# A scheduled attention-and-experts kernel: the loop's head moved behind all scatters, half of the early low parts on GpSimd, the last block closed tile by tile, and other due times

## The chip, the core and the metric

The kernel runs on one core of a Trainium2 chip. The core has a matrix engine (TensorE, PE in the profile; PEld is its loading of weights), a vector engine (DVE), a scalar engine (ACT), GpSimd (POOL) and a queue engine for transfers (SP). Times are device microseconds of the core; the figure that counts is the median of several runs. One execution more is taken with the hardware profiler, and all rows below come from it.

## The reference

Attention over 8 batches of 576 positions with 8 heads of 64, where four heads see a local window and four see a stride of 32; then a mixture of 8 experts over the 4608 rows of 512, each row going to one expert:

```
scores = scale * q @ k.T                      # (8, 8, 576, 576), scale = 1/8
masks  = (0 <= rel < 32) for heads 0..3;  (rel >= 0 and same position mod 32) for heads 4..7
attn   = softmax(where(masks, scores, -1e9)) @ v
x      = attn as 4608 rows of 512
expert = argmax(x @ w_gate);  gate = its softmax probability
out[row] = gate * (relu(x[row] @ w1[expert]) @ w2[expert])   # w1 512x1024, w2 1024x512
```

Everything is float32. A product is made of three matmuls on a high and a low part of each factor (hi*hi, hi*lo, lo*hi), so weights and rows are first split into a high part (a cast on ACT) and a low part (a subtraction).

## The kernel before

**Attention.** Each batch has five banks of scores, 40 in all. A bank goes from PE (mask and scores, `mask`, `scores`) to DVE (`big`, `minus`), ACT (`expo`), DVE (`total`), GpSimd (`norm`, line 664), back to PE (`turned`, four transposes) and to ACT (`out_`); then PE multiplies with v (`av_mm`) into the PSUM banks v and w. Two batches form a group of 9 row tiles. Of each group the gate logits are made (`logit_ops`, whose copy `ev`, line 822, is on DVE), each row tile is transposed and written to a DRAM table xd (`row_ops`, through the PSUM tags in `XTAGS`), and `route_ops` makes the lists of rows of each expert, whose last matmuls are `lists`.

**Experts.** `window` is one block: some 128-row tiles of one expert, gathered from xd by indirect DMAs of GpSimd, transposed on PE into a bank (`tr`, line 421, four transposes of a column of tiles, one after another in `vtags`), split by ACT (`hi`, tile xh) and DVE (`lo`, tile xl), multiplied with w1 (`mm1`, lines 449 to 451, eight steps j of 12 matmuls), relu on ACT (hh), its low part on DVE (hl), multiplied with w2 (`mm2`, lines 469 to 471) into one bank per tile, scaled by the gate (`fin`, tiles y) and written to the output rows by an indirect DMA of GpSimd (`scatter_rows`, line 347, with a one-element memset ahead of a scatter that follows another). A chunk of weights (`weights`) is a load of 1 MB on SP, then for each of its two halves a cast on ACT (line 330) and a subtraction on DVE (line 333, wlo): the first half belongs to w1, the second to w2.

Four early blocks (`PHASES`: experts 0, 2, 4, 6, two tiles each) take rows of the first two groups, and their work lies between the banks of the second half of the attention. After the last group come `make_ids`, `slot_tables` (DVE, lines 1057 to 1087) and the lists of extra tiles ("slots", eight planned by `SLOTS`), then the late blocks of experts 0 to 7 (two or four tiles each) with the slots between them. A slot uses the bank v for its transposes (line 1156), as the late blocks do. At the end a loop takes whatever slots are left over (here it runs no turn).

**What sets the order.** Every piece of work is an `Op` with an engine, a cost, dependences, buffers (`Token`s) and a due time `pri`. `Plan.run` lays them out greedily: for each engine it takes, of the operations that could start within `LOOK` of the earliest, the one with the smallest due time (a PE operation of another tile form counts `FORM_COST` later). Due times come from the constants at the top: `PACE` and `PACE2` for the banks, `LEAD` for loads, `WLEAD` and `WSPL` for weights and their splits, `GLEAD` for gathers, `TLEAD` for a block's transposes, `SLOTP` and `BASEP` for slot tables and late blocks. The order so found is what each engine runs; on the chip an engine takes its instructions in that order and waits at each for its semaphores.

Of the kernel before, what the change touches and what calls it, by code (L numbers as in the profile page):

```python
# [7 lines left out]
F32 = mybir.dt.float32  # L8
# [34 lines left out]
XTAGS = ("yy", "yy", "vw", "vw")  # L43
# [5 lines left out]
PACE = 5.69  # L49
PACE2 = 4  # L50
LAG = 5.0
LEAD = 48.87
ROWLAG = 2.0
FILL0 = 4.87
FILLW = 40.13
WLEAD = 20.91
WSPL = 3.63
SLOTP = 1987.69
BASEP = 2000.0
GLEAD = 38.84  # L60
TLEAD = 22.28
# [38 lines left out]
FORM_COST = 1.14  # L100
LOOK = 0.3
# [17 lines left out]
class Plan:  # L119


    def __init__(self, bufs):
# [12 lines left out]
        self.hold = True  # L135

# [3 lines left out]
    def add(self, eng, cost, fn, deps=(), pri=0.0, take=(), give=(), form=FULL, nbytes=0, rate=380e3, ins=1):  # L140
# [66 lines left out]
    def run(self, held=False):  # L207
# [5 lines left out]
        for op in ops:  # L213
            for d in op.deps:
# [7 lines left out]
        while must:  # L222
# [26 lines left out]
            for s in op.succ:  # L249
                s.left -= 1  # L250
                if s.left == 0:
                    s.at = max(d.done for d in s.deps)
                    avail[s.eng].append(s)
# [15 lines left out]
def moe_attn(ctx, tc, lqk, vl, sqk, vs, wg, wcat, blob, out):  # L269
# [14 lines left out]
                 "route": 1, "sl": 2, "xge": 4, "xe": 1, "ye": 2, "xgm": 9, "xtm": 2, "yp": 5, "sx": 2, "shr": 2, "shh": 2,  # L284
# [76 lines left out]
    def weights(source, deps, pri, pools, after_row=None):  # L361
# [11 lines left out]
        ld = add(SP, 0.45, load, deps, pri, take=[traw], nbytes=128 * CHW * 4)  # L373
        parts = []
        for h in range(2):
# [12 lines left out]
            d = add(DVE, 1.23, lo, [a], pri + WLEAD - WSPL + 0.2 * h, give=[traw])  # L388
# [3 lines left out]
    def window(e, nt, idc, odc, deps, pri, pace, gp, xp, yp_, names, pools, rows=N + 1, width=512, vtags="vw", ytags=YTAGS):  # L392
# [6 lines left out]
        for t in range(nt):  # L399
# [6 lines left out]
            gs.append(add(POOL, 1.0, g, deps, pri - GLEAD, take=[tk], nbytes=128 * XW * 4, rate=250e3))  # L406
# [3 lines left out]
        for dc in range(4):  # L410
# [18 lines left out]
            p = before = add(PE, 0.109 * nt, tr, gs + [before], pri - TLEAD + 2.5 * dc, take=[tv] + ([txx] if dc == 0 else []), ins=2 * nt)  # L429
# [4 lines left out]
        prev = []  # L434
        last = None
        for c in range(NCH):
            p0 = pri + 2 * c * pace
            w, parts, twhl = weights(lambda e=e, c=c: wcat[(e * NCH + c) * 128:(e * NCH + c + 1) * 128, :], (), p0 - WLEAD, pools)
            for fl in range(2):
# [22 lines left out]
                def mm2(w=w, fl=fl, j=j, b=b):  # L462
# [3 lines left out]
                    for t in range(nt):  # L466
                        ts = slice(t * 128, (t + 1) * 128)
                        yb = st["yb"][t]
                        nc.tensor.matmul(yb, b["hh"][:, ts], w["hi"][:, s], start=(j == 0), stop=False)  # L469
                        nc.tensor.matmul(yb, b["hh"][:, ts], w["lo"][:, s], start=False, stop=False)  # L470
                        nc.tensor.matmul(yb, b["hl"][:, ts], w["hi"][:, s], start=False, stop=(j == 7))  # L471

                m1 = add(PE, 12 * mm, mm1, los + [parts[0]], pri + j * pace, take=[tt], give=[txx], ins=24)
                r = add(ACT, act_cost(n), relu, [m1], pri + j * pace, take=[th])
                d = add(DVE, dve_cost(n), rest, [r], pri + j * pace, give=[tt])
                last = add(PE, nt * 3 * 0.229, mm2, [d, parts[1], last], pri + (j + 1.5) * pace, take=ty if j == 0 else (),
                           give=[th, twhl], ins=6 * nt)
        for t in range(nt):
# [11 lines left out]
            f = add(eng, 0.69 if eng == DVE else 0.62, fin, [last], pri + 8 * pace - 8, take=[tk], give=[ty[t], tg[t]])  # L490
# [6 lines left out]
    with ExitStack() as actx:  # L497
# [310 lines left out]
        def logit_ops(g, c3, p):  # L808
# [11 lines left out]
            def ev():  # L820
                st["ls"] = rt.tile([128, 384], F32, name="ls", bufs=2)
                nc.vector.tensor_copy(out=st["ls"], in_=st["lb"][:, 0:384])
# [27 lines left out]
            a = add(DVE, 0.56, ev, [a], p, take=[tls], give=[tb1])  # L850
# [40 lines left out]
        def route_ops(g, p, reds):  # L891
# [47 lines left out]

            def am_():  # L940
# [431 lines left out]
```

## Time and profile before

| | |
|---|---|
| median of three runs | 713.14 us (711.83 to 713.17) |
| profiled execution, its time | 707.22 us |
| profiled execution, span from first to last instruction | 705.4 us |
| PE busy in the span | 642.0 us, 91% |
| DVE, ACT, POOL busy | 449.0, 350.6, 149.2 us |
| mean granted TensorE clock | 0.954 of full speed |

The engine with the largest busy share is PE. A matmul's end in the profile is modelled, so PE's busy time is read for where it is missing: a stretch's idle time of PE and the share of the clock that was granted in it (a level of 0.5 is 1.2 GHz, 1.0 is 2.4 GHz) say what the stretch loses.

### The profile page before, as it was taken

How to read it: one execution, taken by the hardware profiler on the slowest of the kernel's cores; microseconds unless marked ns; L12 is line 12 of the kernel's file. 1: busy time of each engine (PE TensorE's matmuls, PEld its weight loads, DVE VectorE, ACT ScalarE, POOL GpSimd, SP SyncE). 2: the span in 40 equal slices, each digit the busy share in tenths (PEclk: the TensorE clock that was granted, in tenths of full speed). 3: DMA queues.
4: the chain of work that ended last, by engine and by line, in shares of the span. 5: the costliest groups of instructions: out<-in, count | busy, mean ns of one | idle time of the engine just before them, and what ended most of it. 6: DMA issues, size and time to landing. Idle time of an engine off the chain costs nothing. (4 is left out here: it accounts for less than half of the span.)

```text
span 705.4 us, 16723 instructions
## 1 busy us (share of the span) xinstructions
PE 642.0 (91%) x7013; PEld 542.1 (77%) x7020; DVE 449.0 (64%) x791; ACT 350.6 (50%) x601; POOL 149.2 (21%) x189
## 2 busy tenths in 40 slices
PE   5788879799999888999999999999799999999991
PEld 3666656688788677988888888888698888898880
DVE  4576867664886769995455676566477555687110
ACT  2454555355475654464444665446366555676110
POOL 1222321410322414110102403021502200332002
PEclk9699999699999999999999999999899999999996
DMA  9887666826574466576344859565655854592001
GB/s 348 348 304 287 219 234 206 292 102 219 198 257 160 150 258 250 207 261 250 129 178 165 291 200 341 207 238 199 238 179 196 295 196 168 185 369 86 15 1 61
DMA packets 31949, 149.65 MB, mean 212 GB/s; under 512 B 4861, under 2 KB 4861, under 8 KB 21632
## 3 DMA queue, kind: packets, MB, share of 16 engines
q1 hardware_dynamic: 19584, 118.24, 46.5%
q0 software_dynamic: 6432, 20.26, 8.1%
q10 hardware_dynamic: 5856, 10.07, 3.8%
q8 instruction: 56, 0.92, 0.5%
q14 instruction: 21, 0.17, 0.1%
HBM read 129.38 MB, written 20.22 MB: 212 GB/s over the span
## 5 line engine op out<-in xcount | busy, mean ns | idle before, releaser
L333 DVE TENSOR_TENSOR wlo<-raw,whi 128x1024 fp32r<-128x1024 f32 x160 | 195.0, 1235 | 53.8 <-ACT whi L330 53.3
L330 ACT CAST whi<-raw 128x1024 fp32r<-128x1024 f32 x160 | 164.6, 1048 | 22.3 <-PE y L471 10.9
L449 PE MATMUL t<-xh,whi 128*128 128x256 f32 (+1 forms) x384 | 127.3, 332 | 0.0
L451 PE MATMUL t<-xh,wlo 128*128 128x256 f32 (+1 forms) x384 | 123.0, 320 | 0.0
L450 PE MATMUL t<-xl,whi 128*128 128x256 f32 (+1 forms) x384 | 122.6, 319 | 0.0
L456 ACT ACTIVATE hh<-t 128x256 fp32r<-128x256 f32 (+1 forms) x96 | 43.7, 456 | 121.1 <-PE t L451 112.2
L459 DVE SCALAR_TENSOR_TENSOR hl<-t,hh 128x256 fp32r<-128x256 f32 (+1 forms) x96 | 48.5, 508 | 77.4 <-ACT hh L456 77.0
L469 PE MATMUL y<-whi,hh 128*128 128x512 f32 x192 | 79.4, 414 | 2.0 <-ACT hh L456 2.0
L450 PEld LDWEIGHTS t<-xl,whi 128*128 128x128 f32 x384 | 73.3, 191 | 5.9
L449 PEld LDWEIGHTS t<-xh,whi 128*128 128x128 f32 x384 | 73.2, 191 | 6.0
L451 PEld LDWEIGHTS t<-xh,wlo 128*128 128x128 f32 x384 | 73.1, 190 | 5.7
L471 PE MATMUL y<-whi,hl 128*128 128x512 f32 x192 | 76.1, 396 | 0.5 <-DVE hl L459 0.5
L470 PE MATMUL y<-wlo,hh 128*128 128x512 f32 x192 | 75.5, 393 | 0.0
L664 POOL TENSOR_TENSOR prob<-prob,ri 128x512 f32<-128x512 f32 x40 | 43.2, 1083 | 141.6 <-DVE ri L660 70.1
L347 POOL DMA_INDIRECT out_dram<-y,soids x8 | 11.5, 1439 | 205.2 <-DVE y L357 204.9
L643 DVE TENSOR_REDUCE nm<-s 128x8 f32<-128x512 f32 x40 | 27.3, 683 | 34.2 <-PE s L618 23.2
L471 PEld LDWEIGHTS y<-whi,hl 128*128 128x128 f32 x192 | 36.2, 188 | 9.8 <-DVE hl L459 1.5
L347 POOL DMA_INDIRECT out_dram<-y,oids x24 | 29.9, 1245 | 57.4 <-DVE y L357 43.5
L469 PEld LDWEIGHTS y<-whi,hh 128*128 128x128 f32 x192 | 36.2, 189 | 7.6 <-ACT hh L456 2.2
L470 PEld LDWEIGHTS y<-wlo,hh 128*128 128x128 f32 x192 | 36.4, 190 | 5.5
L652 ACT ACTIVATE prob<-prob 128x512 f32<-128x512 f32 x40 | 25.4, 634 | 27.2 <-DVE prob L648 26.1
L327 ACT COPY pT<-t 128x512 f32<-128x512 f32 x40 | 23.0, 590 | 29.0 <-PE t L670 27.0
(166 smaller groups left out, 1255.1 us busy)
## 6 DMA issues: line engine op xcount, KB each, us to landing
raw<-in_wcat_dram SPq DMA_DIRECT2D x80, 1024.0 KB, 5.4
xd<-xr ACTq DMA_DIRECT2D x36, 264.0 KB, 4.4
lqk_sb<-in_lqk_dram SPq DMA_DIRECT2D x16, 592.0 KB, 6.4
sqk_sb<-in_sqk_dram SPq DMA_DIRECT2D x16, 576.0 KB, 6.1
vt<-in_vl_dram SPq DMA_DIRECT2D x16, 576.0 KB, 6.6
vst<-in_vs_dram SPq DMA_DIRECT2D x8, 704.0 KB, 4.6
xg<-xd,ids POOLq DMA_INDIRECT x24, 4.5
out_dram<-y,oids POOLq DMA_INDIRECT x24, 5.0
```

Source lines behind the costliest of these rows:

```text
L330: nc.scalar.copy(out=hi, in_=src)
L333: nc.vector.tensor_tensor(out=lo, in0=src, in1=hi.bitcast(F32), op=ALU.subtract)
L347: i = nc.gpsimd.indirect_dma_start(out=out, out_offset=bass.IndirectOffsetOnAxis(ap=idc, axis=0), in_=y, in_offset=None, bounds_check=N - ...
L449: nc.tensor.matmul(hb[:, 0:n], w["hi"][:, s], xh[:, dc, :], start=(dc == 0), stop=False)
L450: nc.tensor.matmul(hb[:, 0:n], w["hi"][:, s], xl[:, dc, :], start=False, stop=False)
L451: nc.tensor.matmul(hb[:, 0:n], w["lo"][:, s], xh[:, dc, :], start=False, stop=(dc == 3))
L456: nc.scalar.activation(out=b["hh"][:, 0:n], in_=b["hb"][:, 0:n], func=AF.Relu)
L459: nc.vector.scalar_tensor_tensor(out=b["hl"][:, 0:n], in0=b["hb"][:, 0:n], scalar=0.0, in1=b["hh"][:, 0:n].bitcast(F32), op0=ALU.max, op1= ...
L469: nc.tensor.matmul(yb, b["hh"][:, ts], w["hi"][:, s], start=(j == 0), stop=False)
L470: nc.tensor.matmul(yb, b["hh"][:, ts], w["lo"][:, s], start=False, stop=False)
L471: nc.tensor.matmul(yb, b["hl"][:, ts], w["hi"][:, s], start=False, stop=(j == 7))
L664: nc.gpsimd.tensor_tensor(out=pv, in0=pv, in1=st["ri"].unsqueeze(2).broadcast_to([128, 8, 64]), op=ALU.mult)
```

## The change

Named pieces, in the order of the diff:

- Other numbers in the table of due times, `FORM_COST` and `LOOK`; `XTAGS` now puts every group's row transposes on the banks v and w, where groups 0 and 1 used the two y banks.
- Operations may be given a `row`: those of one row keep the order in which they are added (gathers of one pool, loads of one pool, transposes, `mm1`, `mm2`).
- In `weights`, a half that is named in `side` has its low part made on GpSimd; the early blocks name the second half (`EARLY_SIDE = (1,)`). That is one half of each of 16 chunks.
- In `window`, the block of expert 7 has `tail=True`: its last two `mm2` steps (j = 6 and 7) are laid out tile by tile, and a tile's scaling waits for its own last matmul only.
- The logits' copy goes to ACT (`LS_ENG`). `POOL_ROUTES` is empty, so the edits in `route_ops` only divide `bb_` in two.
- Slots gather into a pool of their own (`xgs`, 2 buffers); `xgm` has 7 buffers where it had 9.
- A late block that follows an early expert's block (experts 1, 3, 5, 7) transposes through the banks v, s, s, v and not through v alone.
- `region.close()` stands behind the loop, so the region in which the order is set by hand takes in the loop too.

```diff
-XTAGS = ("yy", "yy", "vw", "vw")
+XTAGS = ("vw",) * 4
...
-PACE = 5.69
-PACE2 = 4
+PACE = 5.08
+PACE2 = 4.89
...
-WSPL = 3.63
-SLOTP = 1987.69
+WSPL = 0.6
+SLOTP = 2008.12
...
-GLEAD = 38.84
-TLEAD = 22.28
+GLEAD = 5
+TLEAD = 24.93
+EW = 128 * max(n for _, _, n in PHASES)
+LS_ENG = "ACT"
+POOL_ROUTES = ()
+EARLY_SIDE = (1,)
...
         op.hold = self.hold
+        op.behind = self.last.get(row) if row else None
+        if row:
+            self.last[row] = op
...
-            def lo(sl=sl):
-                split_lo(w["raw"][:, sl], w["hi"][:, sl], w["lo"][:, sl])
+            le = POOL if h in side else DVE
+
+            def lo(sl=sl, le=le):
+                if le == POOL:
+                    nc.gpsimd.tensor_tensor(out=w["lo"][:, sl], in0=w["raw"][:, sl], in1=w["hi"][:, sl].bitcast(F32),
+                                            op=ALU.subtract)
+                    scattered[0] = False
+                else:
+                    split_lo(w["raw"][:, sl], w["hi"][:, sl], w["lo"][:, sl])
...
+                if tail and j >= 6:
+                    steps.append((mm2, d, parts[1], th, twhl))
+                    th.users = nt
+                    twhl.users = 2 * nt
+                    continue
...
+        ends = [last] * nt
+        if tail:
+            for t in range(nt):
+                for k, (mm2, d, part, th, twhl) in enumerate(steps):
+                    last = add(PE, 3 * 0.229, lambda mm2=mm2, t=t: mm2([t]), [d, part, last], pri + 8.5 * pace + 0.1 * t,
+                               give=[th, twhl], ins=6)
+                ends[t] = last
...
-            f = add(eng, 0.69 if eng == DVE else 0.62, fin, [last], pri + 8 * pace - 8, take=[tk], give=[ty[t], tg[t]])
+            f = add(eng, 0.69 if eng == DVE else 0.62, fin, [ends[t]], pri + 8 * pace - 8, take=[tk], give=[ty[t], tg[t]])
...
-    xgm = ctx.enter_context(tc.tile_pool(name="xgm", bufs=9))
+    xgm = ctx.enter_context(tc.tile_pool(name="xgm", bufs=7))
+    xgs = ctx.enter_context(tc.tile_pool(name="xgs", bufs=2))
...
-               bpools[:1] if ns else bpools, vtags="v")
+               bpools[:1] if ns else bpools, vtags="vss" if 0 < ENT.get(e - 1, 0) else "v", tail=e == E - 1)
...
     plan.run()
-    region.close()
 
     nslots = nc.values_load(nsl[0:1, 0:1], min_val=0, max_val=MAXSLOT)
     with tc.For_i(RSLOT, nslots, 1) as s:
...
         scatter_rows(y, cols[1])
+    region.close()
```

**Place A, the late block of expert 4 among the work of expert 3 and the slots, PE.** In the order before, its first two transposes (line 421, tiles of xg into v) stand around those of a slot (line 1156), all three in the one bank v:

```order
L1217 MATMUL w_6579<-whi_6675,shl_6784 128x512
L421 MATMUL v_6824<-cst_82,xg_6280 128x128
L421 MATMUL v_6824<-cst_82,xg_6803 128x128
L1156 MATMUL v_6839<-cst_82,xg_6810 128x128 x4
L421 MATMUL v_6860<-cst_82,xg_6280 128x128
L421 MATMUL v_6860<-cst_82,xg_6803 128x128
L1187 MATMUL t_6863<-whi_6745,sxh_6837 128x256
```

In the changed kernel the block's first transposes (line 437) are followed by 18 matmuls before a slot's (line 1198), and those by 12 before the block's next; the first fence is the block's first, the second the slot's:

```order
L467 MATMUL t_6639<-xh_6000,wlo_6576 128x512
L437 MATMUL v_6660<-cst_82,xg_5928 128x128
L437 MATMUL v_6660<-cst_82,xg_6291 128x128
L1257 MATMUL w_6606<-whi_6532,shh_6633 128x512
L1258 MATMUL w_6606<-wlo_6533,shh_6633 128x512
```

```order
L1231 MATMUL t_6674<-whi_6630,sxl_6315 128x256
L1198 MATMUL v_6693<-cst_82,xg_6555 128x128 x4
L485 MATMUL y_6323<-whi_6430,hh_6599 128x512
L486 MATMUL y_6323<-wlo_6431,hh_6599 128x512
L487 MATMUL y_6323<-whi_6430,hl_6600 128x512
```

So three uses of the bank v that stood back to back now have matmuls of other blocks between them.

**Place B, the passage from attention to the late blocks, DVE.** Before, `slot_tables` (22 instructions, lines 1057 to 1087) stand ahead of the low parts xl of the early block of expert 6, whose four pairs of transposes PE makes without a matmul between; here the last four rows of the tables and what follows:

```order
L1084 TENSOR_SCALAR raw_4627<-raw_4627 128x40
L1085 TENSOR_TENSOR skey_97<-raw_4627 128x40
L1086 TENSOR_SCALAR raw_4627<-raw_4627 128x40
L1087 CAST srow_96<-raw_4627 128x40
L333 TENSOR_TENSOR xl_4667<-v_4668,xh_4666 128x256
L333 TENSOR_TENSOR xl_4667<-w_4674,xh_4666 128x256
L459 SCALAR_TENSOR_TENSOR hl_4651<-t_4605,hh_4650 128x256
```

In the changed kernel the same 22 instructions (lines 1099 to 1129) stand later, between the low parts hl of two steps of that early block:

```order
L1127 TENSOR_TENSOR skey_97<-raw_4783 128x40
L1128 TENSOR_SCALAR raw_4783<-raw_4783 128x40
L1129 CAST srow_96<-raw_4783 128x40
L475 SCALAR_TENSOR_TENSOR hl_4815<-t_4770,hh_4814 128x256
L342 TENSOR_TENSOR wlo_4818<-raw_4710,whi_4817 128x1024
L342 TENSOR_TENSOR xl_4821<-v_4822,xh_4820 128x256
```

What now waits behind the tables is hl of the step that PE made as t_4770 (and the first xl of the late block of expert 0), where it was the four xl of expert 6.

**Place C, the end of the program, POOL.** One piece of the difference; the rows with + are the changed kernel's last scatters and the loop's head, those with - the order before, where two scatters stand behind the loop's code. The gather and the scatter of a "dyn" tile are the loop's body:

```order
-L1256 COMPARE_AND_BRANCH
-L1256 UNCONDITIONAL_BRANCH
-L347 DMA out_dram<-y,oids 4608x512
-L346 MEMSET gap 1x1
-L347 DMA out_dram<-y,oids 4608x512
-L1368 UNCONDITIONAL_BRANCH
-L1368 ISA
```

```order
+L355 MEMSET gap 1x1
+L356 DMA out_dram<-y,oids 4608x512
+L1296 TENSOR_LOAD nsl
+L1297 COMPARE_AND_BRANCH
+L1297 ISA
+L1297 UNCONDITIONAL_BRANCH
```

The last two scatters moved from behind the loop to ahead of its head.

## Rows read from the trace of the kernel before

**Rows 1.** The page's first part: busy us, share of the span, instructions.
```profile
PE 642.0 (91%) x7013; PEld 542.1 (77%) x7020; DVE 449.0 (64%) x791; ACT 350.6 (50%) x601; POOL 149.2 (21%) x189
```

**Rows 2.** Table by stage: stretch, length, busy by engine, PEclk granted, DMA.
```profile
7.00:140.00 133.00, 107.60 (x2825) 85.02 (x2827) 93.09 (x231) 60.70 (x128) 36.84 (x49) 0.87 0.78 281
140.00:240.00 100.00, 96.40 (x1641) 79.67 (x1647) 69.55 (x153) 58.74 (x118) 23.31 (x33) 0.99 0.52 179
240.00:285.00 45.00, 39.59 (x306) 33.48 (x307) 35.56 (x91) 22.59 (x41) 16.55 (x22) 0.92 0.70 254
285.00:490.00 205.00, 204.18 (x1181) 176.90 (x1180) 135.10 (x170) 107.72 (x163) 30.06 (x31) 1.00 0.60 218
490.00:505.00 15.00, 9.23 (x46) 7.98 (x45) 8.29 (x11) 7.14 (x11) 11.50 (x13) 0.77 0.86 298
689.80:705.40 15.60, 0.02 (x1) 0.00 (x0) 0.13 (x1) 0.69 (x1) 3.18 (x7) 0.57 0.18 69
```

**Rows 3.** Timeline of the last stretch, all engines: start, us, instruction, [idle before].
```profile
685.00 0.69 DVE L459 SCALAR_TENSOR_TENSOR hl<-t,hh 128x512 fp32r<-128x512 f32 x1 [4.84 <-ACT hh L456]
...
688.98 0.39 PE L469 MATMUL s<-whi,hh 128*128 128x512 f32 x1
...
689.44 0.39 PE L471 MATMUL s<-whi,hl 128*128 128x512 f32 x1
...
689.86 0.69 ACT L355 ACTIVATE y<-s,xg 128x512 f32<-128x512 f32 x1 [0.67 <-PE s L471]
690.13 0.97 POOL L347 DMA_INDIRECT out_dram<-y,oids  x1 [0.22 <-DVEq L1256]
...
695.68 0.97 POOL L347 DMA_INDIRECT out_dram<-y,oids  x1 [4.50 <-issue]
...
696.96 0.97 POOL L347 DMA_INDIRECT out_dram<-y,oids  x1 [0.23 <-issue]
```

**Rows 4.** The chain that ended last, by start: the landing, the loop head's last wait.
```profile
690.13 3.66 DMA out_dram<-y,oids
...
694.80 0.12 issue
```

**Rows 5.** Instructions of line 1368, the program's end: ns min/median/max.
```profile
L1368 POOLq DRAIN  x3: 40/109/8602, 696.0 to 705.2; - x3
```

**Rows 6.** Timelines of PE, DVE and ACT at 489 to 506 us.
```profile
492.85 0.38 PE L421 MATMUL v<-cst,xg 128*128 128x128 f32 x2
497.60 1.12 PE L1156 MATMUL v<-cst,xg 128*128 128x128 f32 x4 [4.37 <-DVE xl L333]
500.12 0.69 PE L421 MATMUL v<-cst,xg 128*128 128x128 f32 x2 [1.40 <-DVE sxl L333]
...
493.72 3.49 DVE L333 TENSOR_TENSOR wlo<-raw,whi 128x1024 fp32r<-128x1024 f32 x3
...
492.24 2.92 ACT L330 CAST whi<-raw 128x1024 fp32r<-128x1024 f32 x3
```

**Rows 7.** Timelines of PE and DVE at 255 to 281 us.
```profile
274.46 0.44 PE L421 MATMUL v<-cst,xg 128*128 128x128 f32 x2 [2.66 <-DVE xl L333]
...
268.49 0.17 DVE L1057 TENSOR_SCALAR raw<-cnt 128x8 f32<-128x8 f32 x1
...
273.89 0.18 DVE L1087 CAST srow<-raw 128x40 int32<-128x40 f32 x1
```

**Rows 8.** Groups by shape of wlo and norm; then timelines of POOL and DVE.
```profile
L333 DVE TENSOR_TENSOR wlo<-raw,whi 128x1024 fp32r<-128x1024 f32 x160 | 195.0, 1235 | 53.8 <-ACT whi L330 53.3
L664 POOL TENSOR_TENSOR prob<-prob,ri 128x512 f32<-128x512 f32 x40 | 43.2, 1083 | 141.6 <-DVE ri L660 70.1 <-ACT xT L327 38.5 <-ACT hh L456 6.1
...
217.69 1.05 POOL L664 TENSOR_TENSOR prob<-prob,ri 128x512 f32<-128x512 f32 x1 [4.96 <-ACT whi L330]
...
217.89 1.92 DVE L333 TENSOR_TENSOR wlo<-raw,whi 128x1024 fp32r<-128x1024 f32 x1
```

**Rows 9.** Groups by shape: the eviction of the row transposes.
```profile
L327 ACT COPY xr<-y 128x512 f32<-128x512 f32 x18 | 10.6, 587 | 8.7 <-PE y L874 4.7 <-ACT xr L327 1.9 <-POOL xr L868 0.9
```

More of the change, by code (lines that the diff above doesn't have):

```diff
@@ L99 @@
 FULL, T32, T64, TG = (128, 128), (64, 32), (64, 64), (128, 32)
-FORM_COST = 1.14
-LOOK = 0.3
+FORM_COST = 2.76
+LOOK = 0.19
 class Op:
@@ L213, in run @@
         for op in ops:
-            for d in op.deps:
+            for d in op.deps + ([op.behind] if op.behind else []):
                 if d.done is None:
@@ L251, in run @@
                 if s.left == 0:
-                    s.at = max(d.done for d in s.deps)
+                    s.at = max([d.done for d in s.deps], default=0.0)
                     avail[s.eng].append(s)
@@ L359, in moe_attn, with weights @@
     turn = [0]
-    def weights(source, deps, pri, pools, after_row=None):
+    def weights(source, deps, pri, pools, side=()):
         w = {}
@@ L404, in g @@
                 st["xg"][t] = gather(gp(), idc(t), rows)
-            gs.append(add(POOL, 1.0, g, deps, pri - GLEAD, take=[tk], nbytes=128 * XW * 4, rate=250e3))
+            gs.append(add(POOL, 1.0, g, deps, pri - GLEAD, take=[tk], nbytes=128 * XW * 4, rate=250e3, row=gname))
         txx = token(xname, 8)
@@ L433, in window @@
         mm = n * 0.00044 + 0.004
-        prev = []
+        steps = []
         last = None
@@ L437, in window @@
             p0 = pri + 2 * c * pace
-            w, parts, twhl = weights(lambda e=e, c=c: wcat[(e * NCH + c) * 128:(e * NCH + c + 1) * 128, :], (), p0 - WLEAD, pools)
+            w, parts, twhl = weights(lambda e=e, c=c: wcat[(e * NCH + c) * 128:(e * NCH + c + 1) * 128, :], (), p0 - WLEAD, pools, side)
             for fl in range(2):
@@ L465, in mm2 @@
                     s = slice(1024 + fl * 512, 1024 + fl * 512 + 512)
-                    for t in range(nt):
-                        ts = slice(t * 128, (t + 1) * 128)
+                    for t in ts:
+                        k = slice(t * 128, (t + 1) * 128)
                         yb = st["yb"][t]
[L469 to L473, printed above, removed]
+                        nc.tensor.matmul(yb, b["hh"][:, k], w["hi"][:, s], start=(j == 0), stop=False)
+                        nc.tensor.matmul(yb, b["hh"][:, k], w["lo"][:, s], start=False, stop=False)
+                        nc.tensor.matmul(yb, b["hl"][:, k], w["hi"][:, s], start=False, stop=(j == 7))
+                m1 = add(PE, 12 * mm, mm1, los + [parts[0]], pri + j * pace, take=[tt], give=[txx], ins=24, row="mm1")
                 r = add(ACT, act_cost(n), relu, [m1], pri + j * pace, take=[th])
                 d = add(DVE, dve_cost(n), rest, [r], pri + j * pace, give=[tt])
-                last = add(PE, nt * 3 * 0.229, mm2, [d, parts[1], last], pri + (j + 1.5) * pace, take=ty if j == 0 else (),
-                           give=[th, twhl], ins=6 * nt)
+                if tail and j >= 6:
[3 more added lines that the diff above has]
+                    continue
+                last = add(PE, nt * 3 * 0.229, lambda mm2=mm2: mm2(range(nt)), [d, parts[1], last], pri + (j + 1.5) * pace,
+                           take=ty if j == 0 else (), give=[th, twhl], ins=6 * nt, row="mm2")
+        ends = [last] * nt
[5 more added lines that the diff above has]
+                ends[t] = last
         for t in range(nt):
```

64 lines of the change are left out of this document (38 added, 26 removed).

## The prediction

> **What bounds the kernel now.** I read the page first: PE is busy for 642.0 of 705.4 us [rows 1], and no other engine comes near. So the table by stage is next, and in it two things: how long PE stands idle in a stretch, and what share of the clock it was granted [rows 2]. A stretch loses its idle time, and of a granted share below 1 the rest of its length. From 285 to 490 us PE is busy for 204.18 of 205 us at 1.00: nothing is to be had there but by less work, and the change takes no matmul away. The losses lie elsewhere. From 7 to 140 us PE is idle for 25.4 us and loses 133 x 0.13 = 17.3 us to the clock; from 140 to 240, 3.6 and 1.0 us; from 240 to 285, 5.4 and 3.6 us; from 490 to 505, 5.8 and 3.4 us; and the last 15.6 us hold no matmul at all.
>
> Each loss has its own cause. At the end, the timeline shows the last matmul at 689.44 (0.39 us), the last scaling on ACT from 689.86 to 690.55, but of the last four scatters one starts at 690.13 and the next only at 695.68, the last at 696.96 [rows 3]. The chain says why: GpSimd stands in the loop's head, which waits until the scatter of 690.13 has landed, 3.66 us later, and then runs through its checks until 694.92 [rows 4]. After the last scatter (over at 697.93) GpSimd's DRAIN runs on until 696.02 + 8.60 = 704.6 [rows 5], and the span ends 0.8 us later.
>
> At 493 us PE has made two transposes into the bank v and waits 4.37 us for it, then 1.40 us once more [rows 6]: ACT was in three casts of weights (2.92 us) and DVE in three low parts (3.49 us), and the casts and low parts of the transposes stood behind them. When PE goes on, the clock is at 1.2 GHz for a while, the 3.4 us above. Together 9.2 us.
>
> At 271 us PE has made four pairs of transposes and waits 2.66 us: DVE runs through the 22 instructions of the slot tables from 268.49 to 274.07, and the low parts stand behind them. That costs PE 2.66 us idle and a low clock behind it [rows 7].
>
> **The change, part by part.** The sum is made against the profiled execution, 707.2 us. That lies 5.9 us below the median of the runs and below all three of them, so I carry differences in us over, not the level.
>
> *The end.* The last block's 24 last matmuls are the same, in another order. Its third matmul of step 7 needs hl of that step, which DVE has at 685.00 + 0.69 = 685.69; matmuls follow each other there by (689.44 - 688.98) / 2 = 0.23 us, so the row of 24 starts at 689.44 - 23 x 0.23 = 684.15, and as its sixth this one would start at 685.3: PE ends about 0.4 us later, 690.2. The first three tiles are then done 4.1, 2.7 and 1.4 us ahead of PE's end, and their scatters follow in steps of 1.28 us (696.96 - 695.68). The last tile's scaling then ends at about 691.0, and its scatter starts some 0.28 us later (as between a y and its scatter now), at 691.3, where it was 696.96: 5.6 us sooner. What comes behind is not shown by any row. If the drain goes by the last scatter, it ends 6.7 us after that scatter's end, as now, and the end moves by the whole 5.6. If it only covers the landing, then landing (3.66), checks (1.0) and the close (0.8) bring the end to about 697, a gain of 8.4. If it is 8.60 us from wherever it starts, which would be about 696, the gain is 0.3. I take **-5.6**, since all that GpSimd does in it follows its scatters, with -0.3 and -8.4 as ends.
>
> *Place A.* The uses of v that stood back to back now have 18 and 12 matmuls between, at the mean pitch of the full stretch (204.18 / 1181 = 0.173 us) 3.1 and 2.1 us, against a cast and a low part of a quarter of the size of a weights' half, so well under 1.235 us for both when nothing is ahead of them. A weights' low part of 1.235 us can still stand ahead [rows 8]; so of the 9.2 us I leave 1.2: **-8.0**. Ends: -9.2, and -4 if the pieces of weights come in threes again and only the clock's loss goes.
>
> *Place B.* The transposes of expert 6's early block get matmuls between them, but the tables do not vanish: their 5.6 us now stand ahead of hl of a step. From the end of the `mm1` before, PE has one `mm1` and two `mm2` to do, 24 matmuls by 0.173 us and a pair of transposes, about 4.4 us. hl comes after relu and the hl before (about 0.4 each, by the 0.69 of twice the width at 685.00), a low part (1.2), the tables (5.6) and itself (0.4), at 8.0. So what is late next is `mm2`, by 3.6 us; with half of the stretch's 3.6 us of low clock that is 5.4, against 9.0 now: **-3.6**, with 0 and -9.0 as ends.
>
> *Row transposes on v and w.* The 18 row tiles of groups 0 and 1 used banks of their own; now each holds v or w until ACT has copied it out, 0.587 us [rows 9], and the attention's products, which need v and w, may wait. All 18 waiting makes 10.6 us, none 0. PE's own transposes alternate between the two banks as before, so only the turns from rows to products count, perhaps four of them: **+2**.
>
> *Low parts on GpSimd.* DVE loses 16 x 1.235 = 19.8 us of work. GpSimd takes on 16 of 128x1024, by twice the row of 128x512 16 x 2.17 = 34.7 us [rows 8], beside 76.7 us busy in the first 285 (36.84 + 23.31 + 16.55). In the new order all but two of them come after 33 of the 40 `norm`s, so the attention hardly waits behind them. But the trace shows the two engines in each other's way: the low part that started at 217.89 under a `norm` (217.69 to 218.74) took 1.92 us and not 1.235, longer by 0.69 of the 0.85 us that they shared. So what a DVE subtraction shares with GpSimd is mostly lost. The Trainium skill, page "SBUF — State Buffer", section "Who interferes with whom", has it as an exclusive lock: a DVE instruction with two SBUF inputs and a GpSimd instruction that reads SBUF keep each other out for the whole instruction. Row and page agree, and the page speaks against this edit; by its rule DVE could be kept out for the whole 34.7 us and lose 14.9 on balance. A price for GpSimd stands in the "GPSIMD Engine Reference", section 3.1: its subtraction-like `tensor_tensor` takes 1.96 times DVE's time, an estimate of 2.42 us each, and the sum here would not move by it.
> PE waits little for DVE where these lie (3.6 us idle of 100 from 140 to 240), so I take **+1**; ends -3.6 (that idle time gone) and +14.9 (34.7 us locked, 19.8 saved, all of it on PE's path).
>
> *The rest at nothing.* The logits' copy goes from DVE, 70% busy in the first 140 us, to ACT, 46% busy there [rows 2]. Pools for slots' gathers, the `row` order and smaller GLEAD move gathers on GpSimd, which is busy 15% from 285 to 490; cover gone, a gather's wait stands open, and the order keeps them before the scatters that they were before. New PACE and LEAD leave the first 140 us much as they are: before the second `lists` PE turns 25 banks where it turned 23, in a stretch whose waits are chains through DVE, ACT and GpSimd.
>
> Sum: -5.6 - 8.0 - 3.6 + 2 + 1 = **-14.2**; 707.2 becomes 693.0, and the median 713.1 becomes 698.9, which I round to 699.
>
> **The rivals.**
> 1. *All gains at their ends.* The drain covers only the landing, v is never waited for, the passage to the late blocks runs full, GpSimd's help takes the idle time of DVE's waits: -8.4 - 9.2 - 9.0 - 3.6 = -30.2, 683; half way from my sum it is 691. For it: 43 us of loss in the first 140 that a new order could get at. Against: the tables' 5.6 us have to stand somewhere.
> 2. *The other side: the lock.* Each GpSimd low part delays the second half's `mm2` or locks a subtraction on DVE. Its price is up to +14.9; with +10.6 from the row transposes that leaves -5.6 - 8.0 - 3.6 + 14.9 + 10.6 = +8.3, 721. By the lock alone it is -14.2 + 13.9 = 713, so it decides from about 0.95 us lost by each of the 16. For it: the 1.92 us row. Against: in the order only seven `norm`s lie after most of them.
> 3. *The end doesn't shrink, and place A finds another wait.* The drain stays at 8.6 (-0.3), A gives -4: -0.3 - 4 - 3.6 + 3 = -4.9, 708. For it: one row of the drain, which cannot tell what it waits for.
>
> **How the numbers follow.** My forecast has 0.58, with a range of its own from 693 to 706 (the end at -8.4 or A at -4 and the rows at +5). Rival 1 has 0.2, rival 2 0.12, rival 3 0.1. From 685 to 712 leaves out the last of rival 1 (0.05) and most of rival 2 (0.1). A measurement of this kernel tells about 0.2% (1.4 us) from no change. Faster: 0.58 + 0.2 + 0.1 less a part of rival 3, and the mildest of rival 2, 0.86; same 0.04; slower 0.1.
>
> **What would show it.** Last scatter to last matmul about 1.9 us apart, no scatter behind the loop's checks, and the DRAIN's end 6.7 us behind the scatter (-5.6), at the landing, or 8.6 us long. No PE wait over 1.5 us between the late blocks of experts 3 and 5, and 1.00 granted there. One PE wait of 3 to 4 us on an hl behind the slot tables. GpSimd's low parts near 2.2 us, and DVE's longer where they overlap. I am wrong if PE waits for wlo or for v and w in the first 285 us by more than some 5 us beyond now, or if late blocks show new waits where they ran full.

## The result: 0.5 to 1.4% slower, and the profile after

The changed kernel takes 723.95 us (median of four, 723.61 to 724.53), the kernel before 713.15 beside it: a ratio of 1.014 [1.0098, 1.0182]. In a later series (the second of three below) the same two kernels gave 710.56 and 707.10 us, 1.0046 [1.0022, 1.0070]. So the change costs about 0.5 to 1.4%, where the forecast had a gain of 2%. The profiled execution after took 724.53 us over a span of 722.7; the later series' changed kernel is called "after, again" below (span 710.7), and the kernel before, run once more beside the first experiments, "before, again" (span 706.4).

The page's first part, after (busy us, share, instructions; rows 1 answer to it):

```profile
PE 648.6 (90%) x7016; PEld 545.1 (75%) x7020; DVE 429.6 (59%) x763; ACT 356.6 (49%) x613; POOL 184.0 (25%) x200
```

DVE lost 19.4 us of work and GpSimd took on 34.8, as meant. The table by stage, after, and then after, again; it is read beside [rows 2]:

```profile
140.00:240.00 100.00, 94.51 (x1509) 80.16 (x1509) 59.60 (x137) 54.51 (x108) 42.39 (x42) 0.94 0.52 183
240.00:285.00 45.00, 41.06 (x395) 34.69 (x395) 24.90 (x59) 25.78 (x49) 17.61 (x17) 0.96 0.58 210
285.00:490.00 205.00, 191.23 (x1086) 164.85 (x1085) 131.40 (x181) 99.89 (x151) 44.62 (x41) 0.96 0.59 208
490.00:505.00 15.00, 15.00 (x78) 12.54 (x77) 8.26 (x10) 8.37 (x12) 0.00 (x0) 1.00 0.47 161
709.70:722.70 13.00, 0.00 (x0) 0.00 (x0) 0.00 (x0) 0.66 (x1) 1.67 (x3) 0.65 0.15 54
```

```profile
140.00:240.00 100.00, 96.82 (x1601) 82.74 (x1606) 60.60 (x141) 58.40 (x115) 45.98 (x44) 1.00 0.58 204
285.00:490.00 205.00, 192.78 (x1090) 165.92 (x1091) 129.68 (x170) 99.06 (x150) 37.03 (x35) 0.97 0.58 206
490.00:505.00 15.00, 15.00 (x85) 12.82 (x84) 9.02 (x12) 7.39 (x14) 1.71 (x3) 1.00 0.43 152
697.20:710.70 13.50, 0.00 (x0) 0.00 (x0) 0.00 (x0) 0.69 (x1) 1.71 (x3) 0.64 0.15 53
```

Place A is as forecast: from 490 to 505 PE is busy throughout at 1.00, where it lost 9.2 us. But the stretch from 285 to 490, full before, now stands idle for 205 - 192.78 = 12.2 us and loses 205 x 0.03 = 6.2 more to the clock. What ends PE's waits, after (us in total, times, longest):

```profile
PE y L487 <- DVE hl L475: 8.0, 4, 6.2
...
PE v L437 <- DMA xg<-xd,ids: 4.3, 3, 1.9
...
PE y L486 <- POOL wlo L397: 1.6, 1, 1.6
```

The first is place B. The timeline there, after, of GpSimd, DVE and PE:

```profile
279.29 2.38 POOL L397 TENSOR_TENSOR wlo<-raw,whi 128x1024 fp32r<-128x1024 f32 x1
...
294.66 2.35 POOL L397 TENSOR_TENSOR wlo<-raw,whi 128x1024 fp32r<-128x1024 f32 x1
...
279.37 3.39 DVE L342 TENSOR_TENSOR wlo<-raw,whi 128x1024 fp32r<-128x1024 f32 x1 [2.30 <-issue]
...
289.95 0.17 DVE L1099 TENSOR_SCALAR raw<-cnt 128x8 f32<-128x8 f32 x1
...
294.17 2.91 DVE L1122 TENSOR_TENSOR raw<-cst,raw 128x40 f32<-128x40 f32 x1
...
297.86 0.18 DVE L1129 CAST srow<-raw 128x40 int32<-128x40 f32 x1
297.96 0.42 DVE L475 SCALAR_TENSOR_TENSOR hl<-t,hh 128x256 fp32r<-128x256 f32 x1
...
289.83 0.28 PE L467 MATMUL t<-xh,wlo 128*128 128x256 f32 x1
...
291.79 0.40 PE L486 MATMUL y<-wlo,hh 128*128 128x512 f32 x1
298.43 0.80 PE L487 MATMUL y<-whi,hl 128*128 128x512 f32 x1 [6.25 <-DVE hl L475]
```

The tables take from 289.95 to 298.04, 8.1 us and not 5.6, because an instruction of 128x40 elements, 0.20 us long where nothing disturbs it, takes 2.91 us while GpSimd makes a low part. Behind them PE runs at half speed (a `mm2` matmul 0.80 us, 0.40 before the wait; the granted clock is 0.76 from 298 to 310 us). The tables also end later: `srow`, which the slots' lists need, is written by 298.04 us, in the kernel before by 274.07 [rows 7].

The second wait is new. GpSimd and PE, after, where the late block of expert 3 gets its rows:

```profile
405.76 1.00 POOL L356 DMA_INDIRECT out_dram<-y,oids  x1 [0.31 <-DVE y L366]
...
410.26 1.96 POOL L356 DMA_INDIRECT out_dram<-y,oids  x1 [0.24 <-issue]
412.53 0.99 POOL L348 DMA_INDIRECT xg<-xd,ids  x1 [0.30 <-issue]
413.82 0.97 POOL L348 DMA_INDIRECT xg<-xd,ids  x1 [0.30 <-issue]
415.09 1.77 POOL L348 DMA_INDIRECT xg<-xd,ids  x1 [0.30 <-issue]
...
420.64 0.33 PE L437 MATMUL v<-cst,xg 128*128 128x128 f32 x1 [0.78 <-DMA xg<-xd,ids]
422.91 0.33 PE L437 MATMUL v<-cst,xg 128*128 128x128 f32 x1 [1.94 <-DMA xg<-xd,ids]
424.83 0.48 PE L437 MATMUL v<-cst,xg 128*128 128x128 f32 x1 [1.60 <-DMA xg<-xd,ids]
```

Four scatters, from 405.76 to 412.22, stand ahead of the gathers, and a gather's rows are in use only 8.1 to 9.7 us after it is issued (412.53 to 420.64, 413.82 to 422.91, 415.09 to 424.83).

The end, after: the last matmul, the four last scatters, and of line 1410 (the program's end) the DRAIN, ns min/median/max.

```profile
709.25 0.39 PE L487 MATMUL s<-whi,hl 128*128 128x512 f32 x1
...
706.60 0.97 POOL L356 DMA_INDIRECT out_dram<-y,oids  x1 [35.09 <-DVE y L366]
...
710.64 0.97 POOL L356 DMA_INDIRECT out_dram<-y,oids  x1 [0.24 <-ACTq L1297]
```

```profile
L1410 POOLq DRAIN  x3: 40/103/6692, 715.2 to 722.4; - x3
```

The scatters now come as the tiles are done, the last 1.0 us behind PE. But the DRAIN starts only at 715.18, 3.6 us after the last scatter is over (711.61), runs 6.69 us, and the span ends 0.8 later. The 3.6 us between are the loop's head, which waits for the scatters' landing and then runs its checks, as it did in the kernel before [rows 4].

**Where the time went**: 4.2 us between after, again and before, again (710.67 less 706.44; the two are of two series, in which the kernel before agrees within 0.12%). "Over" is a stretch's length less what the matmuls of products in it take at the pitch of the full clock, 0.229 us for 128x512; transposes are not counted. The first stretch has no such figure, since the attention's matmuls have many forms; there the early blocks' steps are taken off, 37 before and 46 after, each of 6 x 0.229 = 1.374 us. The last column is the same cut of the two profiles of the result's own series (705.4 and 722.7 us).

| stretch | before, again | after, again | difference | before to after |
|---|---|---|---|---|
| start to the last `lists` matmul (256.4, 262.6 us), less early steps | 205.6 | 199.4 | -6.2 | +4.4 |
| from there to 340 us (place B), over | 15.5 | 26.6 | +11.1 | +10.2 |
| 340 to 450 us (expert 3's gathers), over | 7.5 | 14.0 | +6.5 | +5.7 |
| 450 to 540 us (place A), over | 14.7 | 8.9 | -5.7 | -6.1 |
| 540 us to the last matmul, over | 7.7 | 8.6 | +0.9 | +5.5 |
| last matmul's end to the end of the span | 15.9 | 13.5 | -2.4 | -2.6 |

Place B, the gathers, place A and the end come out alike in both; the attention and what lies behind 540 us do not.

The profile after lies 12.45 us behind after, again at the last matmul, with the same order. One piece of it is a pause at 183.26 to 186.43 us in which DVE, ACT and PE all stand still; the profile names as its releaser only "remote". Why that series was higher for both kernels, and more so for the changed one, I have not settled.

### The profile page after: what moved, and what is told of

Read it like the earlier page. It is cut to its first block, busy times and chain, and to the rows that moved or that the text cites. A ratio compares the mean times of both kernels' runs of the same rounds, so it can differ in the third digit from the quotient of the medians.

```text
span 722.7 us, 16776 instructions
## 1 busy us (share of the span) xinstructions
PE 648.6 (90%) x7016; PEld 545.1 (75%) x7020; DVE 429.6 (59%) x763; ACT 356.6 (49%) x613; POOL 184.0 (25%) x200
## 4 chain that ended last, share of the span: by engine, by line
PE 29%; issue 20%; DVE 4%; POOL 4%; DMA 3%; ACT 1%; POOLq 0%; DVEq 0%; ACTq 0%
PE t L465 3%; PE t L467 3%; PE t L466 3%; PE y L487 3%; POOL out_dram L356 2%; PE y L485 2%; PE y L486 2%; DMA xg<-xd,ids 2%; POOL xg L348 1%; DVE wlo L342 1%; PE t L1229 1%; PE t L1231 1%; PE t L1230 1%; DMA raw<-in_wcat_dram 1%; PE s L487 1%
## 5 line engine op out<-in xcount | busy, mean ns | idle before, releaser
L342 DVE TENSOR_TENSOR wlo<-raw,whi 128x1024 fp32r<-128x1024 f32 x144 | 177.0, 1241 | 74.4 <-ACT whi L339 67.5
L465 PE MATMUL t<-xh,whi 128*128 128x256 f32 (+1 forms) x384 | 129.1, 336 | 0.0
L467 PE MATMUL t<-xh,wlo 128*128 128x256 f32 (+1 forms) x384 | 124.5, 324 | 0.7 <-DVE wlo L342 0.5
L466 PE MATMUL t<-xl,whi 128*128 128x256 f32 (+1 forms) x384 | 124.2, 323 | 0.0
L465 PEld LDWEIGHTS t<-xh,whi 128*128 128x128 f32 x384 | 75.2, 196 | 6.7 <-PE s L845 0.6
L467 PEld LDWEIGHTS t<-xh,wlo 128*128 128x128 f32 x384 | 74.8, 195 | 6.7 <-DVE wlo L342 0.7
L466 PEld LDWEIGHTS t<-xl,whi 128*128 128x128 f32 x384 | 75.2, 196 | 6.0
L356 POOL DMA_INDIRECT out_dram<-y,oids x24 | 27.4, 1141 | 119.0 <-DVE y L366 110.2
L397 POOL TENSOR_TENSOR wlo<-raw,whi 128x1024 fp32r<-128x1024 f32 x16 | 38.2, 2386 | 34.7 <-ACT whi L339 25.0
```

What stands on the lines that cost most here:

```text
L342: nc.vector.tensor_tensor(out=lo, in0=src, in1=hi.bitcast(F32), op=ALU.subtract)
L356: i = nc.gpsimd.indirect_dma_start(out=out, out_offset=bass.IndirectOffsetOnAxis(ap=idc, axis=0), in_=y, in_offset=None, bounds_check=N - ...
L465: nc.tensor.matmul(hb[:, 0:n], w["hi"][:, s], xh[:, dc, :], start=(dc == 0), stop=False)
L466: nc.tensor.matmul(hb[:, 0:n], w["hi"][:, s], xl[:, dc, :], start=False, stop=False)
L467: nc.tensor.matmul(hb[:, 0:n], w["lo"][:, s], xh[:, dc, :], start=False, stop=(dc == 3))
```

## The experiments

Ratios are to the kernel before, run on the same chip between them (medians 706.28, 707.10 and 706.74 us in the three series, each on another chip). The changed kernel itself was run in the second series alone. So its 1.0046 is set beside ratios of the other two, and a difference of two such ratios is known to 0.4 to 0.6% only; where it matters, the stretches of the traces are set beside it. The expectations of the first series were written with 1.014 in mind, so there the differences from the changed kernel count and not the levels. My theory after the result: the tables' late and locked place and the late gathers cost the time, and the loop's head took the gain at the end. Rivals: GpSimd's low parts by themselves (the forecast's rival 2), the smaller pool of `xgm`, or a series that was unlucky.

**The two kernels again** (no edit).

> The kernel before, unchanged, timed against itself and profiled once more. Its first profile (707.2 us) lies 6 us below its median. If that execution was a lucky one, the new profile lies near 713 and has 5 to 6 us more idle time or low clock of TensorE somewhere before 285 us; if the profiled execution always differs, it lies near 707 again. The ratio should be 1.000 within 0.3%.

> The changed kernel, unchanged, timed beside the kernel before. In its first profile it lost 4 us to a late load of weights at 183 us, 1.2 us at 521 and 4 us at 636 us that the profiles of its three variants with the same order don't show. If those losses belong to the kernel, the ratio is again 1.014 or so and they show up in the new profile. If they came with that series of runs, the ratio is what the variant with earlier gathers has (0.995) plus the gathers' 7 us: 1.003 to 1.007, and the three losses are gone.

Measured: 0.9994 [0.9967, 1.0020] and 1.0046 [1.0022, 1.0070]. The kernel before came out at 708.2 us in the profile and 706.7 in the median: it is the first series' median of 713 that was high. For the changed kernel the second case came true, and the losses at 183 and 636 us are gone. The sign stands, the size is smaller; the first columns of the table above are made of these two.

**Low parts back on DVE**, the order kept: each of the 16 is made by DVE at the place where GpSimd made it.

```diff
-                if le == POOL:
+                if False:
```

> The changed kernel with its order kept, only the 16 low parts of the early blocks run on DVE at the places where GpSimd had them. Theory 'GpSimd holds DVE up': gone are the wait for wlo at 279 us (1.6), the hl behind the long DVE low part (0.9), the 2.7 us by which one slot-table instruction was stretched, and part of the low clock behind them; 716 to 719 us, a ratio to the kernel before of 1.004 to 1.008. Rival 'the order alone': DVE has 16 x 1.24 us more work, what is won is given back, 722 to 726 us (1.012 to 1.018).

Measured 1.0000 [0.9972, 1.0027], below both ranges, as the changed kernel itself was at 1.0046. The longest wait for hl falls from 6.2 to 2.8 us:

```profile
PE y L487 <- DVE hl L475: 3.9, 3, 2.8
```

So the help costs some 0.46% (1.0046 less 1.0000), 3.3 us, with bounds of about 0.1 and 0.8%; the trace agrees, where the stretch of place B is 23.4 us over and not 26.6. It is not all that was lost.

**Tables in four pieces**, the order otherwise kept: `slot_tables` is cut, and a hl or a low part stands between the pieces (`move` takes operations of the finished order, by number, behind another; `Part` is the next piece).

```diff
...
+        move([48, 49], "sm_ sb_", 63)
+        move([58], "mm", 64)
+        move([66, 67], "sm_ sb_", 78)
+        for i in (42, 45, 56):
+            at.insert(at.index(i) + 1, Part)
```

> The changed kernel with its order kept, but the slot tables cut into four pieces with hl and the weights' low parts between, and the first two list steps of the slots one place later. Theory 'the tables stand ahead of hl': the wait of 6.25 us at 292 us falls below 1.5 us, and the low clock from 298 to 310 us goes with it: 7 to 10 us less, 714 to 717 us (1.001 to 1.006). Rival 'DVE is late there anyway, by GpSimd': 3 us less at most, 721 us or more (1.011).

Measured 1.0088 [1.0058, 1.0119], a miss: the wait for hl went and one for a low part, from 289.0 to 292.8 us, came in its place, and the stretch of place B is 27.7 us over, no shorter than 26.6. So the tables' time can't be had by cutting them alone. Two of their instructions met GpSimd's low parts here too: at 284.80 and 288.28 us a TENSOR_TENSOR of DVE took 2.39 us (0.49 elsewhere) and another 2.36 (0.20 elsewhere).

```profile
PE t L472 <- DVE wlo L347: 4.6, 3, 3.8
```

**The four gathers ahead of the scatters**, the order otherwise kept: they move behind the first of the four.

```diff
...
+        move([322, 326, 330, 335], "g g g g", 309)
```

> The changed kernel with its order kept, but the four gathers that stand behind four scatters at 412 to 418 us moved to behind the first of these. Theory 'the gathers are issued too late, since seven buffers let them go only when the block of expert 1 is done': they start 5.4 us sooner, the three waits for xg at 420 to 425 us (5.2 us with the low clock behind) go, 718 to 720 us (1.006 to 1.010). Rival 'they are slow because the queues are full': they land about as late as now, less than 2 us gained, 722 us or more (1.012).

Measured 0.9948 [0.9917, 0.9978], below both ranges: some 0.98%, 6.9 us, less than the changed kernel, where the table has +6.5 for that stretch; in this trace the stretch is 7.0 us over and not 14.0. The table by stage:

```profile
285.00:490.00 205.00, 197.53 (x1138) 170.37 (x1139) 136.32 (x177) 104.36 (x159) 38.29 (x35) 0.98 0.59 211
```

No wait for xg is left there; this one edit makes the changed kernel faster than the one before, by 0.5%.

**Why they were late: the due time or the pool.** First, GLEAD as before for late blocks' gathers alone, laid out anew; then GLEAD as changed, but slots and late blocks sharing nine `xgm` buffers as before, laid out anew.

```diff
-            gs.append(add(POOL, 1.0, g, deps, pri - GLEAD,
+            gs.append(add(POOL, 1.0, g, deps, pri - (38.84 if gname == "xgm" else GLEAD),
```

> The changed kernel with the old GLEAD of 38.84 for the late blocks' gathers alone, seven buffers kept. Theory 'the due time puts the gathers behind the scatters': the buffers are free ahead of the scatters, so three gathers go ahead of them, the waits at 411 to 416 us go, 0.994 to 0.998. Rival 'too few buffers': the gathers stay where they are, 1.003 or more.

```diff
-    xgm = ctx.enter_context(tc.tile_pool(name="xgm", bufs=7))
-    xgs = ctx.enter_context(tc.tile_pool(name="xgs", bufs=2))
+    xgm = ctx.enter_context(tc.tile_pool(name="xgm", bufs=9))
...
-            st["xg"] = gather(xgs, sids[:, s:s + 1], N + 1)
+            st["xg"] = gather(xgm, sids[:, s:s + 1], N + 1)
```

> The changed kernel with the slots' own pool undone: slots and late blocks share nine gather buffers as before; the order of the late blocks is laid out anew. Theory 'seven buffers make the gathers of expert 3 late': they go out some 60 us sooner, the three waits for xg at 411 to 416 us go, ratio 0.994 to 0.998 (the changed kernel has 1.005). Rival 'the slots' gathers then stand behind late blocks': new waits for xg at the slots' transposes, 1.002 or more.

Measured 0.9947 [0.9921, 0.9973] with the due time, 1.0197 [1.0155, 1.0239] with the shared pool. GpSimd with the due time, the gathers ahead of the scatters again:

```profile
396.25 1.56 POOL L348 DMA_INDIRECT xg<-xd,ids  x1 [0.30 <-issue]
398.12 2.03 POOL L356 DMA_INDIRECT out_dram<-y,oids  x1 [0.30 <-issue]
```

Three of the four gathers go ahead of the scatters, but the waits are not all gone, as they were expected to be; one stays:

```profile
PE v L437 <- DMA xg<-xd,ids: 2.9, 1, 2.9
```

It is for the gather of 396.25, whose rows are in use at 406.29, 10.0 us later, though none of the four scatters stands ahead of it (the two gathers before it land after 3.4 and 7.6 us). So what the moved gathers gain is their earlier issue; their way can be as long as behind the scatters, and what makes it long no run here tells. The stretch from 340 to 450 us is 11.8 us over in this trace, 2.2 less than in after, again; where the rest of the 0.99% comes from is not shown.

PE's waits with the shared pool; those for rows of late blocks are still there, with another of 3.1 us, and a slot waits too:

```profile
PE v L437 <- DMA xg<-xd,ids: 7.8, 4, 3.1
...
PE v L1197 <- DMA xg<-xd,sids: 4.2, 1, 4.2
```

So GLEAD = 5 is what puts the gathers behind the scatters: with the old due time three of them go ahead, though the pool still has seven buffers, and with nine shared ones and GLEAD = 5 they stay behind four scatters.

**Both edits**, gathers moved and low parts on DVE.

> The four gathers moved up as before, and the 16 low parts on DVE too, order kept. Apart, the gathers gave 0.995 and the low parts on DVE 1.000. Theory 'GpSimd's low parts hold DVE up' (lock and late wlo): the two gains add, 0.988 to 0.992. Rival 'the low parts cost nothing': the ratio stays at 0.994 to 0.997; rival 'DVE needs the relief': above 0.997.

Measured 0.9888 [0.9851, 0.9924], as the theory had it: the gains add (0.46 and 0.60% for the low parts, without and with the gathers; each is a difference between two series).

**Gathers moved, tables earlier**: two pieces of the tables ahead of a hl, and the cast and the low part that they wait behind moved up.

```diff
...
+        move([322, 326, 330, 335], "g g g g", 309)
+        move([28], "hi", 25)
+        move([32], "lo", 28)
+        move([35], "slot_tables", 32)
+        at.insert(at.index(35) + 1, Part)
+        at[at.index(29) + 1:at.index(29) + 1] = [Part, Part]
```

> The gathers moved up, and the slot tables split in four and moved ahead: the cast and low part that hold their buffer go ahead of one relu and one hl, the first two pieces follow at once, the other two stand behind that hl. In the variant with the gathers alone TensorE waits 5.5 us for hl at 284 us. Theory 'DVE idles 3 us just ahead of the tables, and only the order puts them late': the wait falls under 1.5 us with no new one of more than 2 us by 340 us, ratio 0.986 to 0.990. Rival 'DVE is full there, as the split tables suggest, so that the wait only moves to a weights' low part': 0.992 or more.

Measured 0.9880 [0.9859, 0.9902], as expected by the ratio; but a wait of 4.6 us for hl stayed, where less than 1.5 was expected, so the ratio came out right without its reason. GpSimd and DVE show why the wait stayed:

```profile
277.80 2.52 POOL L402 TENSOR_TENSOR wlo<-raw,whi 128x1024 fp32r<-128x1024 f32 x1
...
286.45 2.35 POOL L402 TENSOR_TENSOR wlo<-raw,whi 128x1024 fp32r<-128x1024 f32 x1
...
278.10 2.24 DVE L1108 TENSOR_SCALAR raw<-cnt 128x8 f32<-128x8 f32 x1
...
285.88 2.97 DVE L1141 CAST srow<-raw 128x40 int32<-128x40 f32 x1
```

In each of the three places tried, GpSimd's low parts meet the tables; here a TENSOR_SCALAR of 128x8 takes 2.24 us where it takes 0.17 by itself, and a CAST of 128x40 takes 2.97 where it takes 0.18.

**That, with the low parts on DVE** (the edit of the first experiment on top of the last).

> Gathers up, tables split and early, and the 16 low parts on DVE. With GpSimd's low parts kept, the early tables were stretched from 278 to 289 us by two of them (one table instruction took 2.24, another 2.97 us), and TensorE still waited 4.6 us. Theory 'the lock, not the order, holds the tables': without GpSimd's low parts they take some 6 us, the wait for hl near 284 us falls under 2 us, ratio 0.984 to 0.988 (gathers and low parts on DVE gave 0.989). Rival 'DVE's added 19.8 us fill the place': the wait stays at 4 us or more, 0.989 or above.

Measured 0.9843 [0.9803, 0.9884], 698.08 us, as the theory had it: the lowest ratio of all, ahead of both kernels. DVE and the table by stage:

```profile
276.25 0.17 DVE L1108 TENSOR_SCALAR raw<-cnt 128x8 f32<-128x8 f32 x1
...
281.80 0.18 DVE L1141 CAST srow<-raw 128x40 int32<-128x40 f32 x1
```

```profile
285.00:340.00 55.00, 49.19 (x322) 42.28 (x322) 42.69 (x64) 27.09 (x42) 10.38 (x10) 1.00 0.60 210
285.00:490.00 205.00, 199.19 (x1150) 171.06 (x1150) 131.56 (x171) 104.81 (x160) 34.48 (x34) 1.00 0.60 213
```

The tables are back at 5.7 us with a hl between them, no wait for hl is over 0.8 us, and the clock stays at 1.00. Of the idle time left 3.6 us are one wait of a slot for its rows, at 319 us.

**The end: no loop**, which leaves out the loop over left-over slots (here it runs no turn).

```diff
-    nslots = nc.values_load(nsl[0:1, 0:1], min_val=0, max_val=MAXSLOT)
-    with tc.For_i(RSLOT, nslots, 1) as s:
...
-        scatter_rows(y, cols[1])
     region.close()
```

> The changed kernel without the loop for left-over slots (it runs no turn here, so nothing else is left out). Theory 'GpSimd's closing DRAIN takes 6.69 us from when GpSimd gets to it, and the loop's head, which waits for the last scatter to land, stands ahead of it': the DRAIN starts at the last scatter's end and not 3.6 us later, the stretch from the last matmul to the end shrinks from 13.1 to about 9.5 us, ratio 0.005 under that of the changed kernel. Rival 'the DRAIN only waits for the landing': it then lasts 10.3 us, and nothing is gained.

Measured 0.9974 [0.9951, 0.9998], 0.72% under the changed kernel in the same series where 0.5% was expected; the last scatter and the end:

```profile
692.83 0.97 POOL L356 DMA_INDIRECT out_dram<-y,oids  x1 [0.24 <-ACT y L364]
```

```profile
L1361 POOLq DRAIN  x3: 40/107/7905, 692.6 to 701.0; - x3
```

The DRAIN ends at 692.59 + 7.91 = 700.50, 6.70 us behind the scatter's end at 693.80. From the last matmul to the end it is 9.5 us, as expected, 4.0 less than with the loop. The other 1.7 us of the 5.7 between the medians lie inside the interval.

**The end: the kernel before with `region.close()` behind the loop**, nothing else.

```diff
     plan.run()
-    region.close()
...
         scatter_rows(y, cols[1])
+    region.close()
```

> The kernel before with the region's end moved behind the loop, nothing else. Theory from the two DRAINs (6.69 us from GpSimd's last work, and ahead of it the loop's head, which lets GpSimd through some 4 us after the last scatter starts to wait for its landing): the last scatter starts 4.3 us sooner, the DRAIN 3.6 to 4 us later behind it, so the end stretch of 15.8 us shrinks by 0.3 to 0.7 us only; ratio 0.998 to 1.001. Rival, my forecast: all scatters ahead of the head bring 4 us or more, 0.994.

Measured 0.9966 [0.9939, 0.9992], a gain between what the two theories gave; the interval reaches both. The last scatter and the end:

```profile
693.13 0.97 POOL L347 DMA_INDIRECT out_dram<-y,oids  x1 [0.23 <-issue]
```

```profile
L1368 POOLq DRAIN  x3: 40/103/6692, 696.7 to 703.9; - x3
```

The scatters no longer wait in the loop's head (693.13 is the last, 697.94 in before, again), but the head still waits behind them, until 696.68. In before, again the DRAIN's 6.69 us count from the last scatter's end, 698.91; here from 696.68, 2.2 us sooner. From the last matmul to the end it is 13.9 us, 1.9 less than in before, again. In the changed kernel it is 13.5 and 13.1 in its two profiles, so closing the last block tile by tile adds 0.4 to 0.9, little more than the two profiles differ by (not tried by itself).

## Why the prediction was wrong

The sum was -14.2, and the table above has +4.2. Of the 18.4 us between them, place B is 14.7 (+11.1 for -3.6), the gathers 6.5 (for nothing), the end 3.2, place A 2.3 and the rest of the late blocks 0.9; the attention gave back 6.2, and the +3 for row transposes and low parts are inside these stretches. The result's own series had +17.2, 13 us more: the attention is 10.6 higher there (+4.4 for -6.2), what lies behind 540 us 4.6, and the rest 2.2 lower. But for the pause of 3.2 us the cause of that stays open. The forecast also took a measurement to tell 0.2%; the intervals here reach 0.2 to 0.4% to either side, and the ratio of the same two kernels came out 0.9% apart in two series.

- **Place B, the step that failed most**: "hl ... at 8.0", and "one `mm1` and two `mm2` to do, ... about 4.4 us". hl came 8.3 us behind the `mm1`, as said, though by a longer table (8.1 for 5.6) and less ahead of it. But PE had no `mm1` there and only 8 matmuls of `mm2`, where the sum counted 24: one step of 6, a pair of transposes and the first two of the step that needs hl, from 290.1 to 292.2 us. That is 2.1 us of cover and not 4.4, so 6.2 of wait and not 3.6. And I priced the one wait: the kernel also met GpSimd's low parts there (a wait of 1.6 for wlo, and 3.39 us for a DVE low part), and lists that were written late (srow at 288.9 us in after, again, at 275.6 in before, again; that this cost time is not shown). With tables early and low parts on DVE that stretch runs at 1.00. How the 11.1 us split is shown in part, by what the stretch is over in each trace: 26.6 in after, again and 23.4 with the low parts on DVE; with the gathers moved 25.6, with the low parts on DVE besides 22.6, with the tables early 23.6, with both 19.2. So the low parts take 3.0 to 4.4 us and the tables' place 2.0 to 3.4, where the profiles of one order differ by up to 1.2. The last 3.7 us above the kernel before are left, about as much as the slot's wait of 3.6.
- **"the order keeps them before the scatters that they were before"**: wrong, and shown to be. GLEAD = 5 put the gathers of expert 3's late block behind four scatters; either moving them or giving back the due time alone is worth 0.98 to 0.99%, 6.9 us, though only the first shows as much in its own stretch (7.0 us, against 2.2). I had looked at how busy GpSimd is (15%), where the place in its queue counts.
- **The end**: -5.6 came out as -2.4. "If the drain goes by the last scatter" was the mechanism, and 6.7 us behind GpSimd's last work is right. But its last work is now the loop's head, which ends 3.6 us behind the last scatter; my sum let the head vanish. Without the loop the forecast's 6.7 are there (6.70).
- **Place A**: the 9.2 us of the row are gone; over the wider stretch from 450 to 540 it is -5.7 for -8.0, since a slot now waits 2.3 us for low parts (after, again, until 527.65). The four variants with low parts on DVE, cut tables, moved gathers and no loop don't have that wait; there the stretch is 6.6 to 7.3 us over and not 14.7, so the mechanism and the size of this term were right.
- **GpSimd's low parts**: mechanism right, size off. +1 was taken, 3.3 to 4.2 measured (0.46 and 0.60%), inside the bounds of -3.6 to +14.9. Rival 2 named it, but it isn't what turned the sign: without it the changed kernel is at 1.0000. One takes 2386 ns:

```profile
L397 POOL TENSOR_TENSOR wlo<-raw,whi 128x1024 fp32r<-128x1024 f32 x16 | 38.2, 2386 | 34.7 <-ACT whi L339 25.0 <-PE t L467 5.0 <-issue 4.6
```

  The sum had 2.17. The estimate of 2.42 from the Trainium skill's "GPSIMD Engine Reference", section 3.1, was nearer, and the trace agrees with it within 2%.
- **Row transposes**: +2 forecast; PE's waits behind `xr` on v and w are 3.3 us (1.5, 0.9 and 0.9) for 0.6 before: +2.7.
- **The attention at nothing**: in after, again it got 6.2 us shorter for its work, which is a gain that the forecast doesn't have. All ten later traces of the changed attention lie between 195.9 and 203.6, three of the old one between 204.1 and 205.6; the first profile after, at 208.5, does not show it. The experiment with the low parts on DVE has it too (198.7), so it isn't GpSimd's help; which of the due times, the banks or the logits' copy on ACT did it, no run here tells.

## What to carry to other kernels

A queue that is 15% busy can still be late: when due times change, look up at each block what its gathers now stand behind, not how idle the engine is. When work moves, price the new place with the matmuls that really stand between, counted in the order, and with what else runs on an engine that shares its ports. A loop that runs no turn still costs its head's waits at the program's end; see whether what comes last counts from the work or from that head.

## What the runs showed that I had not expected

- In these four kernels GpSimd's closing DRAIN ends 6.69 us (6.70 without the loop) behind GpSimd's last work, whether that is a scatter or the loop's head: from the last scatter's end in the kernel before (697.93 to 704.62) and without the loop (693.80 to 700.50), from the end of the loop's head where that comes later (715.18 to 721.87; 696.68 to 703.37).
- While GpSimd subtracts 128x1024 numbers (2.4 us), even one-input instructions of DVE are held up: a TENSOR_SCALAR of 128x8 for 2.24 us, a CAST of 128x40 for 2.97. I had weighed two-input subtractions alone. The Trainium skill, page "SBUF — State Buffer", section "Who interferes with whom", lists `cast` and `tensor_scalar` among the operations that can take the shared pair of ports, and the trace agrees.
- Near 400 us an indirect gather's rows are in use only 8 to 10 us after its issue, behind four scatters (8.1 to 9.7) and ahead of them (up to 10.0) alike; the median from issue to landing of all such gathers is 4.5 us in the kernel before.
